# Another order of load and cast for the last four batches of an attention-then-MLP kernel

## The chip, the cores and the metric

One Trainium2 chip, one core. The metric is the device time of one execution in microseconds (us); the median over runs is compared. The engines are TensorE (PE in the profile, with its weight loads as PEld), VectorE (DVE), ScalarE (ACT), GpSimd (POOL) and SyncE (SP), whose instructions here are DMA issues. Each engine executes its own instructions in order.

## The reference

```
q, k, v: (8 batches, 8 heads, 576 tokens, 64) f32
scores = q @ k^T / 8                        # per batch and head
D[i, j] = gamma_h ** (i - j) if i >= j else 0,   gamma_h = 1 - 2 ** (-5 - h)
attn = (scores * D) @ v
x = attn.transpose(0, 2, 1, 3).reshape(4608, 512)
h = x @ w_in                                # 512 -> 2048
g = gelu_tanh(h)
out = g @ w_out                             # 2048 -> 512, f32
```

## The kernel before

The attention is computed chunk by chunk with a running state, in f16. From each batch 512 of its 576 tokens are taken in the main flow, as four chunks of 128; the last 64 tokens of every batch, the *tails*, are taken in pairs of batches and make up the ninth and last tile of the dense part. The dense part works on tiles of 512 tokens: tile t (0 to 7) is the main part of batch t, tile 8 the tails. Both dense products use a seven-product scheme on halves of the matrices, so sums of activations and weights (`x_sums`, `act_sums`) run on VectorE.

All engines' programs are written out in a fixed order by hand. A tile is a list of steps for TensorE, and `at(t, u, f)` hangs other work on step u of tile t. Three batches are in work at a time: during tile t,

- the dense layers run for batch t (`up`, `up_prod` for the first layer, `prod` for the second);
- batch t + 1 goes through attention (`scores`, `outs`); `put` copies the result from PSUM to xT, the input of tile t + 1. For the second half of the batch these copies are made on ScalarE at step 24 (line 579);
- batch t + 2 is cast from f32 to f16 in tiles whose size is one 128-token chunk of k, q or v. `parts(b)` gives the order of the 12 casts, and the list `ut` their steps, [16, 16, 17, 18, 18, 19, 20, 20, 21, 22, 22, 25]. k and q are cast on GpSimd (lines 303 and 284), v on ScalarE (line 278) for batch 4 and later. Ahead of the first one, GpSimd makes a one-element copy `gate` (line 1148) that waits for VectorE's sums of this tile. At step 24 `turn_dma` issues two DMA transposes on SP (line 333): first of all k, then of all q, into `tt`, which the scores of the next tile read. In tiles 3 to 5 the casts of k and q of a pair of tails and their own DMA transpose (line 268) follow.

The loads have one queue, SP, in the order of the list `seq`. `pump` issues from it as long as one of the `LD` = 10 staging buffers is free, and each cast frees one. A token `("h",)` at the end of a batch holds the queue until step 29 of the tile (`resume`), so that in SP's order the loads of the next batch stand behind the turns and the stores of the tile. With 10 buffers and 12 loads in a batch, the last two loads are issued only after two casts. A token `("t", b)` loads a pair of tails (`load_tails`, line 96): six DMAs of 128 KB, two each for k, q and v, into three buffers of their own. It needs no staging buffer. k and v are read in runs of 64 elements, q in runs of 128.

For tiles 2 to 5 the loads of batches 4 to 7 thus stand in SP's program as 12 loads (k0, q0, v0, k1, ... v3), then (tiles 3 to 5) the six tail loads, then the turn of k, the turn of q, the turn of the tails, and two stores of the output (line 817).

Of the kernel before, what the change touches and what calls it, by code (L numbers as in the profile page):

```python
# [20 lines left out]
def kernel(  # L21
# [11 lines left out]
    B, H, S, D = q.shape  # L33
# [95 lines left out]
    def parts(b):  # L129
        if b == NPE:  # L130
            return [(key, c) for key in "kqv" for c in range(NC)]
        return [(key, c) for c in range(NC) for key in "kqv"]

    def body(b):
        if b < NPE:
            return [("b", b, key, 2 * g + y) for g in range(2) for key in "qkv" for y in range(2)]
        return [("b", b, *x) for x in parts(b)]

    QS = (0, 2, 1, 3)
    seq = body(0) + [("i", g, ct) for g in QS for ct in range(4)]  # L140
    seq += [("o", f) for f in range(NF)] + body(1)
    TP = {4: 0, 5: 2, 6: 4, 7: 6}
    for b in range(1, B):
        seq += body(b) if b > 1 else []
        if b - 1 in TP:
            seq.append(("t", TP[b - 1]))
        if NPE <= b < 8:
            seq.append(("h",))
    q_ld = {"next": 0, "hold": False}
# [972 lines left out]
    for t in range(1, B):  # L1122
        b, tl = t + 1, TP.get(t)
# [12 lines left out]
    for b in range(NPE, B):  # L1136
        ent = parts(b)
        eng = {"k": P, "q": P, "v": P if b == NPE + 1 else A}
        t0, ut, go = b - 2, [16, 16, 17, 18, 18, 19, 20, 20, 21, 22, 22, 25], 29
        if b == NPE + 1:  # L1140
            ut = [16, 16, 17, 19, 19, 20, 22, 22, 23, 24, 24, 25]
        if b == NPE:
            t0, ut, go = 1, [0, 0, 0, 0, 2, 2, 4, 4, 6, 7, 9, 10], 12
        at(t0, ut[0], lambda b=b: (new_casts(b), new_turned(b)))
        if b >= 8:
            at(t0, ut[0], lambda: q_ld.update(hold=True))
        if b > NPE:
            at(t0, ut[0], lambda t=t0: nc.gpsimd.tensor_copy(out=gate, in_=gs[t]["2" if t in MID else "4"][:, NH - 1, 1, 0:1]))  # L1148
        for u, (key, c) in zip(ut, ent):
            at(t0, u, lambda b=b, key=key, c=c, e=eng[key]: cc(b, key, c, e))  # L1150
        at(t0, 5 if b == NPE else ut[-2] + 2, lambda b=b: turn_dma(b, TP.get(b - 1)))
        at(t0, go, resume)
# [105 lines left out]
```

## Time and profile before

The median of three runs is 285.23 us (283.83 to 286.21). The profiled execution took 283.99 us, its span is 282.2 us.

| | |
|---|---|
| PE busy | 271.8 us of the span (96%), 4106 matmuls |
| DVE busy | 234.8 us (83%) |
| ACT busy | 170.5 us (60%) |
| POOL busy | 136.4 us (48%) |
| granted TensorE clock | 0.997 |
| HBM read / written | 36.70 MB / 9.44 MB |
| DMA queue of SP | 126672 packets, 52.97 MB, 76% of 16 engines' span |

A busy share is over the whole span, with a start (the first 24 us, where PE is busy for 19.65) and an end (252.3 to 282.2 us, 25.24) that have other limits than the middle. The chain of work that ended last runs through PE for 69% of the span, DVE 11% and DMA 8%.

### The profile page before, as it was taken

Reading aid. Unit: us, or ns where it says so; the run is one execution under the profiler, and the core shown is the slowest. Engines: PE = TensorE matmul, PEld = TensorE weight load, DVE = VectorE, ACT = ScalarE, POOL = GpSimd, SP = SyncE. Lnnn points to the kernel's source line nnn. Section 1 sums busy time; section 2 is a strip of 40 time slices with the busy share of each in tenths; the row PEclk is TensorE's granted clock in tenths of the full one; section 3 lists DMA queues with packets and bytes.
Section 4 is the critical chain, followed back from the end, with each engine's and each line's share of the span. In section 5 each row is a group of like instructions: output and inputs, shape, how many; then the busy total and the mean of one; then the engine's idle time right before and its main releaser. Section 6 shows DMA issues by size and latency. Waiting matters only on the chain.

```text
span 282.2 us, 9780 instructions
## 1 busy us (share of the span) xinstructions
PE 271.8 (96%) x4106; PEld 214.5 (76%) x4106; DVE 234.8 (83%) x439; ACT 170.5 (60%) x325; POOL 136.4 (48%) x239
## 2 busy tenths in 40 slices
PE   6889999999999999999999999999999999999993
PEld 2458888888877688678867887688668877887782
DVE  6785999998968899779988997899888968875863
ACT  5477756797246864776478646874586368308800
POOL 4589809980893099109950896079717000000000
PEclk9999999999999999999999999999999999999998
DMA  6999999999979982999699999999993040012013
GB/s 196 302 385 385 379 282 242 251 208 282 226 166 264 246 204 56 269 237 222 133 214 251 205 202 194 285 206 199 192 252 68 8 153 0 2 73 78 0 39 112
DMA packets 127307, 54.11 MB, mean 192 GB/s; under 512 B 93472, under 2 KB 119072, under 8 KB 127264
## 3 DMA queue, kind: packets, MB, share of 16 engines
q1 hardware_dynamic: 126672, 52.97, 76.0%
q8 instruction: 32, 0.52, 0.9%
q10 hardware_dynamic: 592, 0.52, 0.6%
q14 instruction: 11, 0.09, 0.1%
HBM read 36.70 MB, written 9.44 MB: 163 GB/s over the span
## 4 chain that ended last, share of the span: by engine, by line
PE 69%; DVE 11%; DMA 8%; POOL 4%; ACT 3%; issue 1%; SPq 1%; DVEq 0%
PE hp L593 11%; PE opB L800 11%; PE opA L800 10%; PE opC L800 9%; PE hB L695 8%; DMA ld<-in_moe_w_in_dram 4%; PE hC L695 4%; PE opD L800 4%; PE xs L428 3%; PE hp L614 3%; POOL w_out_sb L912 2%; DMA ld<-in_q_dram 2%; PE hA L695 2%; ACT gT L710 2%; DMA ld<-in_moe_w_out_dram 2%; DVE ret L372 2%
## 5 line engine op out<-in xcount | busy, mean ns | idle before, releaser
L800 PEld LDWEIGHTS <-gT 128*128 128x128 f16 x576 | 55.0, 98 | 9.2 <-issue 0.8
L593 PE MATMUL hp<-xT,w_in_sb 128*128 128x512 f16 x192 | 49.1, 379 | 0.0
L800 PEld LDWEIGHTS <-s 128*128 128x128 f16 x432 | 42.0, 98 | 5.0
L303 POOL TENSOR_TENSOR ck<-ld,sc 128x128 f16<-128x128 f32 (+1 forms) x72 | 43.2, 626 | 1.2 <-DMA ld<-in_k_dram 0.6
L599 ACT ACTIVATE gT<-hp 128x512 f16<-128x512 f32 x48 | 28.5, 593 | 12.4 <-PE hp L593 8.9
L800 PE MATMUL opA<-w_out_sb,gT 128*128 128x256 f16 x288 | 35.0, 273 | 0.3 <-ACT w_out_sb L912 0.2
L284 POOL TENSOR_TENSOR cq<-ld,sc 128x256 f16<-128x256 f32 x48 | 31.5, 677 | 0.1
L695 PEld LDWEIGHTS <-w_in_sb 128*128 128x128 f16 x256 | 25.1, 98 | 8.2
L614 PE MATMUL hp<-xT,w_in_sb 128*128 128x256 f16 x256 | 29.7, 273 | 1.0 <-POOL w_in_sb L912 0.9
L593 PEld LDWEIGHTS <-w_in_sb 128*128 128x128 f16 x192 | 18.7, 98 | 12.8 <-DVE xT L579 0.2
L614 PEld LDWEIGHTS <-w_in_sb 128*128 128x128 f16 x256 | 24.3, 98 | 5.3 <-POOL w_in_sb L912 2.3
L710 ACT ACTIVATE gT<-k 128x512 f16<-128x512 f32 x25 | 15.8, 631 | 13.2 <-DVE k L706 13.2
L695 PEld LDWEIGHTS <-wi 128*128 128x128 f16 x192 | 18.3, 98 | 5.1
L1148 POOL COPY gate<-s 128x1 f16<-128x1 f16 x5 | 2.5, 492 | 39.1 <-DVE s L777 30.9
L776 DVE TENSOR_TENSOR s<-gT 128x512 f16<-128x512 f16 (+1 forms) x26 | 15.3, 589 | 7.2 <-ACT gT L621 4.5
L621 ACT ACTIVATE gT<-hp 128x512 f16<-128x512 f32 x32 | 18.5, 599 | 4.3 <-PE hp L614 4.1
L579 ACT CAST xT<-xs 128x512 f16<-128x512 f32 x23 | 15.4, 736 | 9.1 <-PE xs L428 9.1
L695 PE MATMUL hC<-x,w_in_sb 128*128 128x256 f16 x128 | 19.2, 273 | 0.0
L695 PE MATMUL hB<-x,wi 128*128 128x256 f16 x128 | 18.9, 273 | 0.0
L800 PE MATMUL opB<-wt,gT 128*128 128x256 f16 x144 | 18.2, 273 | 0.0
L779 DVE TENSOR_TENSOR gT<-gT 128x512 f16<-128x512 f16 (+1 forms) x26 | 17.7, 696 | 0.0
L777 DVE TENSOR_TENSOR s<-s,gT 128x512 f16<-128x512 f16 (+1 forms) x26 | 16.6, 639 | 1.2
(147 smaller groups left out, 566.7 us busy)
## 6 DMA issues: line engine op xcount, KB each, us to landing
ld<-in_q_dram SPq DMA_DIRECT2D x32, 256.0 KB, 5.4
ld<-in_k_dram SPq DMA_DIRECT2D x32, 256.0 KB, 5.7
ld<-in_v_dram SPq DMA_DIRECT2D x32, 256.0 KB, 5.3
out_dram<-ost SPq DMA_DIRECT2D x16, 512.0 KB, 4.6
ld<-in_moe_w_in_dram SPq DMA_DIRECT2D x16, 256.0 KB, 5.5
ld<-in_moe_w_out_dram SPq DMA_DIRECT2D x16, 256.0 KB, 5.7
lt<-in_k_dram SPq DMA_DIRECT2D x8, 128.0 KB, 5.7
lt<-in_q_dram SPq DMA_DIRECT2D x8, 128.0 KB, 4.7
```

The lines of the kernel that those rows point to most:

```text
L284: eng.tensor_tensor(out=a[key][:, 1024 * g + 512 * x : 1024 * g + 512 * x + 512].rearrange("p (n l d) -> p l n d", l=2, d=D)[:, y ^ x], in ...
L303: eng.tensor_tensor(out=dh[:, o], in0=x, in1=sc[:, s0, i].unsqueeze(2).to_broadcast(list(x.shape)), op=ALU.mult)
L579: cp(out=xT[:, g0 : g0 + 4 : 2].rearrange("p g n (t j) -> p g n j t", j=2), in_=t.rearrange("p (n g j t) -> p g n j t", n=HP, g=2, j=2),)
L593: nc.tensor.matmul(hp.rearrange("p (g t) -> p g t", t=TL), w_in_sb[:, ct, 128 * fc : 128 * fc + 128], xT[:, o : o + TB // TL, ct, :], star ...
L599: nc.scalar.activation(out=gT[t][:, fc].rearrange("p i n -> p (i n)"), in_=hp, func=AF.Gelu_apprx_tanh)
L614: nc.tensor.matmul(hps[n][:, 256 * x : 256 * x + 256].rearrange("p (g t) -> p g t", t=TL), w_in_sb[:, ct, 128 * (fs[n] + x) : 128 * (fs[n] ...
L621: nc.scalar.activation(out=gT[t][:, f : f + 2, 2 * u : 2 * u + 2, :].rearrange("p f i n -> p f (i n)"), in_=hp.rearrange("p (f n) -> p f n ...
L695: nc.tensor.matmul(pb[:, 256 * i : 256 * i + 256].rearrange("p (g t) -> p g t", t=TL), w(kt, i), x(kt), start=(new and i == kt == 0), stop ...
L710: due.append(lambda: nc.scalar.activation(out=g, in_=x.rearrange("p (f n) -> p f n", f=2), func=AF.Gelu_apprx_tanh))
L777: nc.vector.tensor_tensor(out=s["2"], in0=s["1"], in1=a11, op=ALU.subtract)
L779: nc.vector.tensor_tensor(out=a21, in0=a11, in1=a21, op=ALU.subtract)
L800: nc.tensor.matmul(op[tag][:, HD * u : HD * u + HD], lhs(f), rhs[:, f], start=(new and f == 0), stop=(f == NH - 1), skip_group_check=True,)
```

## The change

For batches 4 to 7 the order of the 12 loads and casts becomes k0 k1 v0 k2 k3 v1 q0 q1 q2 q3 v2 v3. The steps of the list `ut` are dealt out in that order. The token of the tail loads, which stood behind a batch's last load, is put at the eleventh place of the batch's list, between q3 and v2, for batches 5 to 7 (batch 4 has no tails; the last pair of tails is loaded elsewhere, in tile 6). Order of instructions before and after: on PE, DVE and ACT the same; on SP and POOL regrouped. Line numbers behind the change are higher by 2 or 3.

```diff
     def parts(b):
         if b == NPE:
             return [(key, c) for key in "kqv" for c in range(NC)]
+        if b >= 4:
+            return [(x[0], int(x[1])) for x in "k0 k1 v0 k2 k3 v1 q0 q1 q2 q3 v2 v3".split()]
         return [(key, c) for c in range(NC) for key in "kqv"]
...
     TP = {4: 0, 5: 2, 6: 4, 7: 6}
     for b in range(1, B):
-        seq += body(b) if b > 1 else []
+        new = body(b) if b > 1 else []
         if b - 1 in TP:
-            seq.append(("t", TP[b - 1]))
+            new.insert(10 if b < B else 0, ("t", TP[b - 1]))
+        seq += new
         if NPE <= b < 8:
             seq.append(("h",))
```

The lines of SP's program for batch 5 (tile 3), before and after:

```
before: k0 q0 v0 k1 q1 v1 k2 q2 v2 k3 q3 v3 | tails k k q q v v | turn k, turn q, turn tails | 2 stores
after:  k0 k1 v0 k2 k3 v1 q0 q1 q2 q3 | tails k k q q v v | v2 v3 | turn k, turn q, turn tails | 2 stores
```

## The prediction

> **What bounds the kernel now.** I read the busy table by stage first, then the instruction queues around one tile boundary. In what follows "tile t" is the stage that runs the two dense layers on 512 tokens of batch t; in it batch t+1 goes through attention and batch t+2 is loaded, cast and turned. The change touches batches 4 to 7, so tiles 2 to 5, which begin at 82.5, 111.1, 139.4 and 168.5 us; tile 6 begins at 197.5. The table (columns: length, then PE, PEld, DVE, ACT, POOL busy, granted clock, DMA share, GB/s):
>
> ```profile
> 111.20:139.60 28.40, 28.40 (x454) 21.82 (x452) 24.61 (x41) 18.36 (x35) 15.09 (x26) 1.00 0.93 215
> 139.60:168.50 28.90, 28.83 (x501) 22.36 (x500) 25.64 (x43) 19.04 (x37) 18.56 (x33) 1.00 0.96 213
> 168.50:197.50 29.00, 28.93 (x501) 22.52 (x500) 25.34 (x42) 19.10 (x37) 18.67 (x34) 1.00 1.03 220
> ```
>
> TensorE is never idle here: 28.40 of 28.40, 28.83 of 28.90. With the neighbouring tiles, 82.7 to 226.3 us, the idle time adds up to 0.3 us. So the change has at most 0.3 us to win there, and everything it can do beyond that is harm. The DMA share (0.93 to 1.03) says that the second resource at its limit is the DMA queue. Next, SP's queue in tile 4 (start, length of the issue, what):
>
> ```profile
> 158.15 2.71 SPq L111 DMA_DIRECT2D ld<-in_k_dram  x1
> 160.95 1.28 SPq L106 DMA_DIRECT2D ld<-in_q_dram  x1
> 162.33 0.46 SPq L111 DMA_DIRECT2D ld<-in_v_dram  x1
> 162.84 2.36 SPq L96 DMA_DIRECT2D lt<-in_k_dram  x2
> 165.24 1.31 SPq L96 DMA_DIRECT2D lt<-in_q_dram  x2
> 166.59 1.32 SPq L96 DMA_DIRECT2D lt<-in_v_dram  x2
> 168.07 3.36 SPq L333 DMA_TRANSPOSE tt<-ck  x1
> 171.53 1.99 SPq L333 DMA_TRANSPOSE tt<-cq  x1
> ```
>
> SP issues without a pause from 147.29 (the batch's first load) to 167.9: k3, q3, v3, six tail loads, then the two turns. The first ten loads are out at 160.9; the tails take 5.1 us more. Then ScalarE's timeline over the same boundary:
>
> ```profile
> 163.62 0.61 ACT L278 CAST cv<-ld 128x512 f16<-128x512 f32 x1
> 164.14 1.32 ACT L579 CAST xT<-xs 128x512 f16<-128x512 f32 x2
> 167.33 0.62 ACT L278 CAST cv<-ld 128x512 f16<-128x512 f32 x1 [1.86 <-DMA ld<-in_v_dram]
> 169.42 0.60 ACT L599 ACTIVATE gT<-hp 128x512 f16<-128x512 f32 x1 [1.48 <-PE hp L593]
> ```
>
> This is the view that decides. The cast of v2 (163.62) stands ahead of the two copies that write xT (164.14), and xT is what the first matmul of the next tile reads at 168.47. The cast of v3 already waits 1.86 us for its load (issued 162.33, so 5.0 us from issue to use), harmlessly, because it stands behind the xT copies. The program order of PE, DVE and ACT is the same before and after; only SP's and POOL's orders move.
>
> **The change, part by part.**
>
> *POOL.* The same 8 casts of k and q, regrouped: k first. In tile 4 the four k casts sum to 1.77 + 2.22 + 2.41 + 1.57 = 8.0 us and the four q casts to 5.3 us, behind the gate that ends at 156.6. So k is cast whole at 164.6 in place of 168.05, q at the same 169.5. Cost 0.
>
> *The turn of k.* It waits for k's cast, but on SP it also stands behind the loads of v2 and v3. In tile 4 SP is through with loads and tails at 167.9 in either order, and the turn is issued at 168.07 now. Gain in this tile 0.1 us, in tile 3 about 1.9 us (137.3 for 139.21). The turn of q still waits for the last q cast; its result is needed by scores some 8.6 us into the next tile, for which no PE wait is on record. Worth 0.
>
> *The loads of v2 and v3.* There are 10 staging buffers, so the last two loads of a batch wait for casts. These were q3 and v3; now they are v2 and v3. For tiles 3 to 5 the six tail loads are put ahead of them. The wait on casts (now k0 and k1) costs nothing: in tile 4 these end at 158.3 and 160.6, and also 2.6 us later (the delay worked out below) they are over before SP gets there at 166.0. What counts is the place in the queue: v2 goes from ninth load to eleventh plus six tails.
>
> *Tile 2 (no tails).* Ten loads are out at 102.3 us; v2 is issued then in place of 99.85. Landings in that window take 4.5 to 6.1 us, so it is there at 107.5 (106.8 to 108.4); its cast stands at 106.46 now. The xT copies move from 106.98 to about 108.1 and end at 109.4, before tile 3 starts at 111.1. Cost 0 us, at the worst bound 0 too (110.3); the cover is 1.7 us of ScalarE slack.
>
> *Tile 3.* Ten loads out at 129.5 (q3 is issued at 129.57 now); six tails by the rows of before 131.42 to 137.32, 5.9 us: v2 issued at 135.4. For its landing I take 4.5 us, the middle of the tail rows here (3.7 to 5.2), since it follows them in a queue that they have let drain; loads in the full queue took 4.5 to 5.7. It lands at 139.9. Then the cast (0.6), the two xT copies (1.32) and a hand-over of 0.1: tile 4 starts at 142.0 for 139.4, **+2.6 us**. The four sums of xT on VectorE (0.42 to 0.83 us each) stand behind the same copies and run beside the first matmuls, as they do at the start of tile 2 (83.24 to 85.9), where they cost PE nothing I can see. v3 follows v2 by about 0.7 us and its cast stands behind the copies: 0.
>
> *Tile 4.* Where does the delay go? SP's next loads start after the turn of q (POOL's cast end 140.7, unmoved), the tails' turn and the stores, so still at 147.3. Ten loads to 160.9, tails 5.1, v2 at 166.0, landing 4.6 (tail rows 4.2 to 4.7): 170.6; tile 5 starts at 172.7 for 168.5, **+4.2** in all, of which 1.6 are new.
>
> *Tile 5.* POOL's gate has moved by 2.6 with tile 4, and q's cast with it; SP had 1 us of slack there, so loads start 1.7 us later (178.2). Ten loads took 12.8 us, tails 5.8: v2 at 196.8, landing 4.5, tile 6 at 203.4 for 197.5: **+5.9**. Behind tile 6 no batch is loaded and nothing is given back: PE is busy 28.7 of 28.8 and 25.9 of 26.0 us in tiles 6 and 7.
>
> *Sum.* The profiled execution took 283.99 us (span 282.2 and 1.8 around it): 283.99 + 5.9 = 289.9. The runs' median, 285.23, lies 1.24 above it; the forecast of the median is 289.9 + 1.2 = **291.1 us**.
>
> *Bounds.* The unknowns are how fast the tails go when they come straight behind q3, and the landing of a load behind them. Low rows: 0.60 us for each tail issue (the shortest) and 3.7 us to land. Tile 3: 129.5 + 3.6 + 3.7 = 136.8, copies done 138.8, no loss; tile 4: 168.2, tile 5 starts at 170.3, +1.8; tile 5 adds none: 287.0 for the median. High rows: the issue lengths of before and the longest landings of a load (5.7, 6.7, 6.6): +3.8, +6.3, +9.3 with the loads of tile 5 3 us late: 294.5.
>
> **The rivals.**
>
> *The clock falls in the gaps.* The trace shows what idling costs:
>
> ```profile
> 279.00:280.00 1.00, 0.00 (x0) 0.00 (x0) 0.00 (x0) 0.00 (x0) 0.00 (x0) 1.00 1.01 318
> 280.00:281.00 1.00, 0.00 (x0) 0.00 (x0) 0.00 (x0) 0.00 (x0) 0.00 (x0) 0.83 0.56 176
> 281.00:282.20 1.20, 0.00 (x0) 0.00 (x0) 0.00 (x0) 0.00 (x0) 0.00 (x0) 0.50 0.00 0
> ```
>
> The last matmul ends at 277.66; 0.83 over one us means a drop to 0.50 at about 280.7, 3.0 us later. And a cold start, from PE's timeline:
>
> ```profile
> 2.28 3.57 PE L253 MATMUL fill<-tbb,ident 128*128 128x512 f16 x8 [2.28 <-POOL tbb L209]
> 10.40 1.47 PE L253 MATMUL fill<-tbb,ident 128*128 128x512 f16 x6
> ```
>
> Eight such matmuls took 3.57 us at first; at the later pace (0.245 each) they take 1.96: 1.6 us lost. My gaps are 2.6, 1.6 and 1.7 us, all under 3.0, so the forecast has no drop; with landings at the high rows the first gap is 3.8 and one drop follows, two at most: 294.5 + 1.6 = 296, or about 293.5 with one gap just over 3.0. The Trainium skill ("TensorE: Matmul & The Clock Gate", Part 1: The HAM clock gate) says that the clock is halved after about 3.4 us of idling, judged by a free-running window; the trace's 3.0 us agrees roughly, and by that rule also a gap of 2.6 is spared.
>
> *v2 arrives in time: not slower.* The place is the same, the copies behind v2's cast. What decides is whether v2 lands by 137.3 in tile 3 (tile 4's start of 139.4 less 2.1), 2.6 us earlier than I have it. For: the last tails are issued in 0.60 each, and a q load reads runs of twice the length of a k load's, so ten loads with four q instead of three pass sooner. Against: in all three tiles six tails took 5.1 to 5.9 us. Price as in the low bound, +0 to +1.8: 285.2 to 287.0.
>
> *The regrouping pays.* The turn of k goes out 1.9 us earlier, SP's loads of the next batch follow, and a wait for turned keys falls away. For: the DMA share is near 1. Against: PE has no such wait; the gain is capped at 0.3 us: 284.9.
>
> **How the numbers follow.** The late v2 that I forecast, +3.5 to +9.3, has a chance of 0.70 and its own range is 288.7 to 294.5; late with clock drops 0.12 (293 to 297); in time 0.15; regrouping pays 0.03. A measurement of this kernel tells about 1% (2.9 us) from no change, so slower by over 1% gets 0.82, within 1% 0.15, faster 0.03. The range runs from 286.6 (inside the in-time case) to 295.3 (into the case with the clock).
>
> **What would show it.** Right: in tiles 3 to 5 the cast of v2 on ACT with a wait of 5 to 8 us for its load; the first matmul of the next tile idle until ACT's xT copies, 2.6, then about 1.6 and 1.7 us; nothing of the kind at 111 us; the clock at 1.00 throughout; POOL's and DVE's busy time unchanged. Step by step: v2's issue at 135.4 and 166.0, the tails ahead of it. Wrong: no PE gap at the starts of tiles 4 to 6, or v2 landing under 137.3; a gap at the start of tile 3; or a PE wait on turned tiles or on xT's sums in place of the copies.

## The result and the profile after

The changed kernel takes 287.42 us (median of 12 runs, 286.1 to 291.31) for 284.39 us before (12 runs, 283.13 to 286.21). The ratio is 1.0111 with a 95% interval of 1.0092 to 1.0130: slower by 3.0 us, where +5.9 us was forecast (291.1 us for the median). The run of 291.31 us is taken as a slow one and is left out of the ratio. The profiled span is 284.8 us for 282.2 us.

The busy table by stage, with the cut and the columns shown of before:

```profile
111.20:139.60 28.40, 27.96 (x452) 21.60 (x450) 22.95 (x40) 17.86 (x35) 15.00 (x26) 1.00 0.94 204
139.60:168.50 28.90, 28.47 (x498) 22.00 (x497) 24.39 (x42) 18.57 (x37) 17.53 (x32) 1.00 1.07 218
168.50:197.50 29.00, 28.39 (x496) 21.71 (x495) 24.57 (x42) 17.64 (x35) 17.63 (x32) 1.00 0.97 214
```

TensorE, which had been idle for 0.14 us of these three stretches, is idle for 0.44, 0.43 and 0.61 us in them. The clock stays at 1.00. Cut by tiles instead (from first matmul to first matmul), tiles 2 to 6 take 28.53, 28.79, 29.63, 30.38 and 29.31 us, where before they took 28.54, 28.37, 28.88, 29.00 and 28.81. The differences add up to 3.0 us, the whole loss; tile 2 has no share in it. (The profiled span grew by only 2.6 us, because this execution came to tile 2 0.44 us earlier, at 82.08 for 82.52 us, ahead of everything that the change touches. Points in time after the change, as against those before, are early by that much from the start.)

SP's queue in tile 4, from the q loads on:

```profile
154.01 2.69 SPq L106 DMA_DIRECT2D ld<-in_q_dram  x4
156.75 1.52 SPq L96 DMA_DIRECT2D lt<-in_k_dram  x2
158.31 2.64 SPq L96 DMA_DIRECT2D lt<-in_q_dram  x2
161.06 1.42 SPq L96 DMA_DIRECT2D lt<-in_v_dram  x2
162.58 2.29 SPq L111 DMA_DIRECT2D ld<-in_v_dram  x2
164.96 4.22 SPq L336 DMA_TRANSPOSE tt<-ck  x1
169.44 1.94 SPq L336 DMA_TRANSPOSE tt<-cq  x1
```

The order is the one announced, and everything in it is early: v2 is issued at 162.58, the forecast had 166.0. ScalarE around the starts of tiles 4 (139.40) and 5 (169.03):

```profile
137.52 0.62 ACT L281 CAST cv<-ld 128x512 f16<-128x512 f32 x1 [3.47 <-DMA ld<-in_v_dram]
138.04 1.31 ACT L582 CAST xT<-xs 128x512 f16<-128x512 f32 x2
139.51 0.62 ACT L281 CAST cv<-ld 128x512 f16<-128x512 f32 x1 [0.15 <-DMA ld<-in_v_dram]
140.51 0.60 ACT L602 ACTIVATE gT<-hp 128x512 f16<-128x512 f32 x1 [0.39 <-PE hp L596]
...
143.05 0.63 ACT L713 ACTIVATE gT<-k 128x512 f16<-128x512 f32 x1 [1.24 <-DVE k L709]
...
144.07 0.58 ACT L733 COPY k<-hB 128x512 f32<-128x512 f32 x1
...
167.13 0.62 ACT L281 CAST cv<-ld 128x512 f16<-128x512 f32 x1 [3.39 <-DMA ld<-in_v_dram]
167.66 1.32 ACT L582 CAST xT<-xs 128x512 f16<-128x512 f32 x2
169.55 0.62 ACT L281 CAST cv<-ld 128x512 f16<-128x512 f32 x1 [0.58 <-DMA ld<-in_v_dram]
170.13 0.60 ACT L602 ACTIVATE gT<-hp 128x512 f16<-128x512 f32 x1
```

The cast of v2 waits for its load with the two xT copies behind it, as forecast, but for 3.4 to 4.1 us and not for 5 to 8. And two lines in the middle, the gelu that waits for VectorE and the late copy L733, belong to a second cost that the forecast did not have. TensorE shows both:

```profile
139.40 1.02 PE L596 MATMUL hp<-xT,w_in_sb 128*128 128x512 f16 x4 [0.44 <-ACT xT L582]
...
144.69 0.60 PE L698 MATMUL hB<-x,wi 128*128 128x256 f16 x4 [0.36 <-ACT k L733]
...
174.40 0.60 PE L698 MATMUL hB<-x,wi 128*128 128x256 f16 x4 [0.44 <-ACT k L733]
...
199.41 1.02 PE L596 MATMUL hp<-xT,w_in_sb 128*128 128x512 f16 x4 [0.77 <-ACT xT L582]
...
204.68 0.60 PE L698 MATMUL hB<-x,wi 128*128 128x256 f16 x4 [0.33 <-ACT k L733]
```

The first place is a tile's first matmul, idle until ACT's xT copies: the profile puts 0.44 and 0.77 us down to these copies at tiles 4 and 6. It counts from the end of the matmul before, which is modelled, so the starts of matmuls are the safer measure, and by them the gaps are somewhat longer. The last group of 16 matmuls of a tile starts 2.35, 2.01 and 2.68 us ahead of the next tile, where before it was 1.75. That is 0.60, 0.26 and 0.93 us at the starts of tiles 4, 5 and 6, 1.8 in all. The second place is 5.3 us into tiles 4, 5 and 6: 0.36, 0.44 and 0.33 us by the profile, and by the starts (0.95, 1.04 and 0.93 us from the matmuls before, for 0.44) 0.51, 0.60 and 0.50 us, 1.6 in all. Together this is 3.4 us, 0.4 more than the loss: by difference, the rest of these tiles is 0.4 us shorter than before; why stays open. The second place hangs on the first by a chain through VectorE:

```profile
139.39 0.61 DVE L673 TENSOR_TENSOR x<-xT 128x512 f16<-128x512 f16 x1 [1.45 <-ACT xT L582]
...
142.34 0.67 DVE L709 TENSOR_TENSOR k<-k,hA 128x512 f32<-128x512 f32 x1
```

VectorE stands idle for 1.45 us before the four sums of xT, which began at 138.46 before and at 139.39 now. They run one after the other, then the output sum L817, then L709 (142.34 for 141.87 before). The gelu of L713 needs that sum (143.05 for 142.59), the copy L733 stands behind it (144.07 for 143.60), and that copy frees the bank in which the matmul of 144.69 writes.

### The profile page after: what moved, and what is told of

It reads as the page before. It is cut to its first block, busy times and chain, and to the rows that moved or that the text cites. A ratio compares the mean times of both kernels' runs of the same rounds, so it can differ in the third digit from the quotient of the medians.

```text
span 284.8 us, 9784 instructions
## 1 busy us (share of the span) xinstructions
PE 271.9 (95%) x4106; PEld 213.9 (75%) x4106; DVE 231.5 (81%) x439; ACT 170.3 (60%) x325; POOL 134.3 (47%) x239
## 5 line engine op out<-in xcount | busy, mean ns | idle before, releaser
L306 POOL TENSOR_TENSOR ck<-ld,sc 128x128 f16<-128x128 f32 (+1 forms) x72 | 41.2, 607 | 1.6 <-DMA ld<-in_k_dram 1.5
L713 ACT ACTIVATE gT<-k 128x512 f16<-128x512 f32 x25 | 15.8, 632 | 15.0 <-DVE k L709 15.0
L281 ACT CAST cv<-ld 128x512 f16<-128x512 f32 x22 | 13.7, 623 | 14.8 <-DMA ld<-in_v_dram 14.8
L779 DVE TENSOR_TENSOR s<-gT 128x512 f16<-128x512 f16 (+1 forms) x26 | 14.6, 563 | 6.6 <-ACT gT L624 3.9
L803 PE MATMUL opB<-wt,s 128*128 128x256 f16 x144 | 17.4, 273 | 0.0
```

The costliest lines, as they stand in the source:

```text
L281: eng.copy(out=dst, in_=raw)
L306: eng.tensor_tensor(out=dh[:, o], in0=x, in1=sc[:, s0, i].unsqueeze(2).to_broadcast(list(x.shape)), op=ALU.mult)
L713: due.append(lambda: nc.scalar.activation(out=g, in_=x.rearrange("p (f n) -> p f n", f=2), func=AF.Gelu_apprx_tanh))
L779: nc.vector.tensor_tensor(out=s["1"], in0=a21, in1=a22, op=ALU.add)
L803: nc.tensor.matmul(op[tag][:, HD * u : HD * u + HD], lhs(f), rhs[:, f], start=(new and f == 0), stop=(f == NH - 1), skip_group_check=True,)
```

## The experiments

Theory after the result: the loss comes from v2's cast, which is late and stands ahead of the xT copies in ScalarE's order, and reaches TensorE in two places, directly and through VectorE's sums. Rivals: the reordered loads themselves (DMA or GpSimd contention), and v3's cast, which stands ahead of the next tile's first gelu. Ratios are to the kernel before, with 95% intervals; each diff is to the changed kernel, and `...` stands for code left out.

**e1_tails_last: tails behind v3 again.**

```diff
-            new.insert(10 if b < B else 0, ("t", TP[b - 1]))
+            new.append(("t", TP[b - 1]))
```

> The new order of loads and casts is kept, and only the six tail loads go back behind v3 in SP's queue (tiles 3 to 5). If the loss is v2's load standing behind the tails: v2 is issued right after q3, 6 to 7 us earlier (near 126 and 156 us), its cast on ACT waits for nothing, PE has no gap at the starts of tiles 4 to 6 nor at step 6 of these tiles, and the time is that of before, ratio to before 0.998 to 1.002. If the new order itself costs (v2 and v3 as the last two loads, q casts late), it stays near 1.011; if half and half, near 1.005.

Measured: 284.41 us, 0.9994 [0.9972, 1.0016]. v2 is issued at 130.04, 158.66 and 187.64 in tiles 3 to 5, later than expected (near 126 and 156): in tile 3 SP is through with q3 at 127.22 and stands idle until GpSimd's cast of k0 frees a staging buffer. There is still no gap at either place. The place of the tails accounts for the whole loss; the new order of loads and casts, taken together, costs nothing that these runs resolve.

**e2_v2_behind_copies: v2's cast behind the xT copies on ScalarE.**

```diff
+        if b >= 4:
+            ut = [16, 16, 17, 18, 18, 19, 20, 20, 21, 22, 24, 25]
```

> All loads and their order are as in the changed kernel; only the cast of v2 on ACT is moved from ahead of the two copies to xT to behind them (batches 4 to 7). If ACT's queue is what turns the late load into a loss: v2 lands as late as in the changed kernel (137.5, 167.1, 197.5 us, or somewhat earlier in absolute time as the tiles move up), but PE starts tiles 4 to 6 without a gap, VectorE's sums of xT wait for nothing, the gap at step 6 goes too, ratio to before 0.998 to 1.003. If the loss came from the busier DMA queue or from late turns, the ratio stays near 1.011.

Measured: 285.58 us, 1.0034 [1.0008, 1.0060]. The gaps at the starts of tiles are gone, so the first place is v2's cast ahead of the copies. What is left is a further mechanism: the late casts stand ahead of the next tile's first gelu instead. At the start of tile 5 the casts run at 168.14 and 170.01, the gelu at 170.54, and TensorE waits 0.20 and 0.45 us for the copies that free a bank (L727 and L733). The expectation that the gap 5.3 us into the tile would go too did not hold.

**e3_only_v3_behind: v2 ahead of the tails, v3 behind them.**

```diff
-            new.insert(10 if b < B else 0, ("t", TP[b - 1]))
+            new.insert(11 if b < B else 0, ("t", TP[b - 1]))
```

> The tail loads are put one place later, between v2 and v3: v2 leaves ahead of them, v3 stays behind. If only a load whose cast stands ahead of the copies to xT can hurt: no gap at the tile starts, v3's cast waits 1 to 3 us behind the copies, ratio to before 0.998 to 1.003. If any value load behind the tails costs, about half the loss remains: 1.005.

Measured: 285.93 us, 1.0045 [1.0018, 1.0071]: v3 alone costs something once it comes this late. ScalarE, then TensorE, at the start of tile 5 in this kernel:

```profile
170.36 0.62 ACT L281 CAST cv<-ld 128x512 f16<-128x512 f32 x1 [3.83 <-DMA ld<-in_v_dram]
170.88 0.59 ACT L602 ACTIVATE gT<-hp 128x512 f16<-128x512 f32 x1
171.37 0.58 ACT L727 COPY k<-hB 128x512 f32<-128x512 f32 x1
```

```profile
172.00 0.60 PE L698 MATMUL hB<-x,wi 128*128 128x256 f16 x4 [0.42 <-ACT k L727]
```

The cast waits 3.83 us, the gelu and the copy behind it follow without a pause, and TensorE waits for the bank, and again for 0.45 us at 174.34.

**e4_old_order_tails_first: the old order k0 q0 v0 ..., with the tails ahead of its last two loads.**

```diff
-        if b >= 4:
-            return [(x[0], int(x[1])) for x in "k0 k1 v0 k2 k3 v1 q0 q1 q2 q3 v2 v3".split()]
```

> The old order of loads and casts, with the tail loads ahead of the batch's last two loads (now q3 and v3). This tells the place of the tails from the order. v2 is the ninth load and early, so by the theory of v2 there is no gap at the starts of tiles 4 to 6 from the copies; q3 lands 5 to 6 us later, about when GpSimd comes to its cast (139.2 in tile 3 of before), so the turn of q is up to 2 us later and hidden: ratio 0.998 to 1.004. If tails ahead of the last two loads cost whichever these are, it is near 1.011. The ten loads with three q in them should take 12.5 to 13 us, against 10.9 to 11.5 with four.

Measured: 287.36 us, 1.0099 [1.0063, 1.0134]. The expectation that it would be hidden failed. The last two loads are q3 and v3 here, and v3's cast, harmless behind the xT copies while it waited 1.86 us, now waits 6.27:

```profile
172.89 0.62 ACT L279 CAST cv<-ld 128x512 f16<-128x512 f32 x1 [6.27 <-DMA ld<-in_v_dram]
173.42 0.59 ACT L600 ACTIVATE gT<-hp 128x512 f16<-128x512 f32 x1
173.91 0.58 ACT L725 COPY k<-hB 128x512 f32<-128x512 f32 x1
```

```profile
174.53 0.60 PE L696 MATMUL hB<-x,wi 128*128 128x256 f16 x4 [1.92 <-ACT k L725]
```

A second wait of 0.45 us follows in the same tile, and no tile starts with a gap: v3's place explains the loss here, without the late q3. Tails ahead of the last two loads cost about 1% in either order of the loads.

**e5_late_casts_next_tile: the changed kernel's loads, and the casts of v2 and v3 at step 3 of the next tile.** No cast of a late load then stands ahead of the copies or of the first gelu.

```diff
-            at(t0, u, lambda b=b, key=key, c=c, e=eng[key]: cc(b, key, c, e))
+            t1, u1 = (t0 + 1, 3) if b >= 4 and key == "v" and c > 1 else (t0, u)
+            at(t1, u1, lambda b=b, key=key, c=c, e=eng[key]: cc(b, key, c, e))
```

> Loads and their order as in the changed kernel; the casts of v2 and v3 (batches 4 to 7) move into the next tile on ACT, to step 3, behind the first gelus and copies of that tile; the values are first needed at step 15. Theory now: the late value loads cost at two places of ACT's queue, v2's cast ahead of the copies to xT, and v3's cast ahead of the next tile's first gelu. Moving v2 alone behind the copies left 0.3%. If these two places are the whole loss, no PE gap is left in tiles 4 to 6 and the ratio to before is 0.998 to 1.002. If the tails ahead of the values cost through DMA or turns as well, 1.003 to 1.005 stays.

Measured: 283.96 us, 0.9992 [0.9971, 1.0012]. The whole loss is gone with the same loads in the same order. Its busy table, cut at its own tile starts:

```profile
112.40:140.50 28.10, 28.10 (x454) 21.75 (x452) 23.88 (x41) 18.26 (x35) 14.42 (x26) 1.00 1.06 217
140.50:169.40 28.90, 28.83 (x502) 22.43 (x501) 25.06 (x43) 18.94 (x37) 18.80 (x34) 1.00 0.93 207
169.40:198.40 29.00, 28.92 (x502) 22.32 (x500) 25.30 (x43) 19.05 (x37) 18.49 (x33) 1.00 1.04 219
```

TensorE is idle for 0.15 us of the 86.0, as before the change. That rules out contention from the loads, and any cost from their lateness except through what stands behind the casts.

**e11_only_v3_next_tile: as e5, for v3 alone.**

```diff
-            at(t0, u, lambda b=b, key=key, c=c, e=eng[key]: cc(b, key, c, e))
+            t1, u1 = (t0 + 1, 3) if b >= 4 and key == "v" and c == 3 else (t0, u)
+            at(t1, u1, lambda b=b, key=key, c=c, e=eng[key]: cc(b, key, c, e))
```

> Loads as in the changed kernel; v3's cast moves into the next tile (step 3), v2's stays ahead of the copies to xT. This prices the first of the two places by itself: the PE gaps at the starts of tiles 4 to 6 stay (0.3 to 0.9 us), VectorE's sums of xT still begin late and the gaps at step 6 stay, ratio to before 1.007 to 1.011. If v3's place made more of the loss than v2's, the ratio falls to 1.005 or below.

Measured: 287.44 us, 1.0087 [1.0058, 1.0115]. v2's cast alone makes most of the loss. By the profile, gaps of 0.44, 0.29 and 0.50 us stand at the starts of tiles 4 to 6, and of 0.35, 0.24 and 0.58 at the place 5.3 us in (by the starts, 1.7 us in all at each place). So with v3's cast out of the way, the second place is still there. That it is fed by VectorE's late sums is read from the timelines; no run takes the sums out by themselves. What v3 costs in the changed kernel, 0.24% by the difference, is inside the intervals and not resolved.

**e7_four_more_loads: four more loads of 32 KB behind the tails, ahead of v2.** It makes v2 later and changes nothing else that the forecast counts.

```diff
+        x = sb.tile([128, 256], F32, tag="lx", name="lx", bufs=1) if b < TP[7] else None
+        for n in range(4 if b < TP[7] else 0):
+            nc.sync.dma_start(
+                out=x[32 * n : 32 * n + 32].rearrange("p (h d) -> p h d", d=D),
+                in_=k[b, 0:4, 32 * n : 32 * n + 32, :].rearrange("h s d -> s h d"),
+            )
```

> The changed kernel with four more small loads (32 KB each, into a buffer that nothing reads) behind the tails of tiles 3 to 5, ahead of v2: v2 is issued some 2 to 2.5 us later in each tile, so it lands about where I had forecast. If PE's loss follows v2's landing one for one, the first gap is about 2.6 us, the two others 1.5 to 2 us, span about 2.5 to 4 us longer than the changed kernel's, ratio to before 1.019 to 1.026. If the forecast's sum was wrong in its mechanism (the loss doesn't follow v2), it stays near 1.011 to 1.013.

Measured: 293.35 us, 1.0323 [1.0280, 1.0365].

```profile
143.53 1.02 PE L602 MATMUL hp<-xT,w_in_sb 128*128 128x512 f16 x4 [1.91 <-ACT xT L588]
...
174.17 1.02 PE L602 MATMUL hp<-xT,w_in_sb 128*128 128x512 f16 x4 [1.22 <-ACT xT L588]
...
205.66 1.02 PE L602 MATMUL hp<-xT,w_in_sb 128*128 128x512 f16 x4 [2.14 <-ACT xT L588]
```

Counted from the tile's start, v2's cast stands 1.5, 1.0 and 1.1 us later than in the changed kernel (28.38, 28.76, 29.61 for 26.91, 27.73, 28.50). The idle time before these matmuls, by the starts 2.1, 1.4 and 2.3 us, grew by 1.5, 1.1 and 1.4 us: close to one for one, so the rule of the forecast (a late v2 moves the next tile's start) holds, and from cast to first matmul there are 1.88 us each time. The second place did not grow with it (0.17, 0.17 and 0.23 us by the profile, for 0.36, 0.44 and 0.33). Tiles 3 to 6 took 3.5 us more than in the changed kernel, in the expected range. The whole took 5.9 us more, more than expected. In the profile tile 2 is 1.0 us longer, where the edit adds no load, and the stretch before it 1.6 us, though the start of tile 2 varies as much between kernels that don't touch it (81.8 to 83.7). The clock doesn't explain it in the profiled run (mean 0.999), though it was lower in the three others (0.982 to 0.992). This part stays open.

**e12_four_loads_behind: the same four loads behind v3,** meant as the control.

```diff
+    def load_more(b):
...
+            new.append(("x", TP[b - 1]))
...
-            if s[0] != "t":
+            if s[0] not in "tx":
...
```

> Control for the kernel with four more loads: the same four small loads into the same buffer, but behind v3 in SP's queue, ahead of the turns. v2 lands as in the changed kernel, so by the theory that the loss follows v2 the ratio is 1.009 to 1.015 (some 2 us more SP time ahead of the turns is hidden). If the extra loads or the buffer's place in memory cost by themselves, as the earlier tiles of that kernel hint (tile 2 was 1.0 us longer there, with nothing changed in it), it is near 1.02 or above.

Measured: 289.25 us, 1.0156 [1.0113, 1.0198], somewhat above what was expected. The excess over the changed kernel comes from tile 4 (32.55 us for 29.63): v2's cast waits 6.09 us there, tile 5 begins with a gap of 2.78 us, and the clock falls behind it (last section). The control was not clean. In SP's order the four loads stand ahead of the turns, k's turn goes out at 137.41 for 135.18 in the changed kernel, and tile 4's loads begin 7.1 us into the tile for 6.1.

**e6_casts_alone: loads in the old order, tails last, only the casts regrouped.**

```diff
-        if b >= 4:
-            return [(x[0], int(x[1])) for x in "k0 k1 v0 k2 k3 v1 q0 q1 q2 q3 v2 v3".split()]
...
-            new.insert(10 if b < B else 0, ("t", TP[b - 1]))
+            new.append(("t", TP[b - 1]))
...
-        ent = parts(b)
+        ent = parts(b) if b < 4 else [(x[0], int(x[1])) for x in "k0 k1 v0 k2 k3 v1 q0 q1 q2 q3 v2 v3".split()]
```

> Loads in the old order with the tails last; only the casts are regrouped (k first, then q; v2 at step 22). This tells why the next batch's loads began 1.6 to 1.8 us earlier than I had reckoned. If it is the earlier turn of k that follows from the casts: the turn of k goes out as soon as SP is through with the loads, the turn of q takes about 2 us to issue in place of 3.4 to 4.0, and k0 of the next batch is issued near 115.4 and 145.5 us relative to tile starts as in the changed kernel; ten loads still take 12.5 us or more, as three q are among them. If the early start came from the regrouped loads, it stays near 117 and 147.3. Time as before either way: ratio 0.998 to 1.002.

Measured: 284.80 us, 1.0030 [1.0002, 1.0058]. The time is 0.3% above that of before, more than expected; TensorE waits 0.64 us in tile 3 for the turned q, whose casts stand behind those of k. The early start of the next batch's loads did not come: GpSimd's casts of k wait for their loads (10.2 us in 11 waits), and the loads begin 8.0 and 7.5 us into tiles 3 and 4, for 4.8 and 6.1 in the changed kernel and 5.9 and 7.9 before. So the casts alone don't bring it. In e10 (below), with the loads alone, the loads begin 7.6 us into tile 4, but that kernel is disturbed by other waits; with both (e1) they begin 4.0 and 6.7 us in.

**e10_loads_alone: loads in the new order, tails last, casts in the old one.**

```diff
-            new.insert(10 if b < B else 0, ("t", TP[b - 1]))
+            new.append(("t", TP[b - 1]))
...
-        ent = parts(b)
+        ent = parts(b) if b < 4 else [(key, c) for c in range(NC) for key in "kqv"]
```

> Loads in the new order with the tails last, casts in the old order (v2 at step 21). Counterpart to the kernel with the casts alone: the ten loads with four q among them should go out in 10.9 to 11.5 us, and the next batch's loads should begin late as in before (117 and 147.3 us), because k's cast ends late. One look: span within 1 us of before.

Measured, in a single run: 295.66 us, span 293.9 us, far off the expectation. q0, now the seventh load, is still the second cast: GpSimd waits 3.83 us for it in tile 4 with all later casts of k behind it, and TensorE's small state matmuls wait for k, in tile 2:

```profile
109.48 0.97 PE L431 MATMUL us<-cv,ck 64*64 64x64 f16 x16 [1.70 <-POOL ck L306]
```

Again an in-order engine held up by one late load. The ten loads took 12.5, 13.3 and 11.8 us here, as in the old order, so the order of loads alone doesn't make them faster.

No version here beats the kernel before; TensorE's idle time in these tiles, 0.3 us, left nothing to gain.

## Why the prediction was right and wrong

*Right: what binds.* The direction, the place, the gaps of the first kind in tiles 4 to 6 and none in tile 3, the clock at 1.00. In tile 2 v2's cast came at 107.22 (forecast 107.5), the copies were done at 109.06 and there was no gap. That the time agrees so well is luck: v2 was issued at 100.83 and not at 102.3, and took 6.4 us from issue to cast and not 5.2. e2 and e5 show the mechanism, e7 that it pays about one for one.

*Wrong: the size of the first place, forecast at 5.9 us, measured 1.8.* The failed step is "v2 issued at 135.4" and its like in tiles 4 and 5; the terms of that sum (us; the ten loads' end includes their start):

| | tile 3: forecast, measured | tile 4 | tile 5 |
|---|---|---|---|
| loads begin | 117.0, 115.4 | 147.3, 145.5 | 178.2, 175.2 |
| ten loads out | 129.5, 126.2 | 160.9, 156.8 | 191.0, 186.7 |
| six tails take | 5.9, 7.4 | 5.1, 5.8 | 5.8, 6.5 |
| v2 issued | 135.4, 133.66 | 166.0, 162.58 | 196.8, 193.24 |
| issue to cast | 4.5, 3.9 | 4.6, 4.6 | 4.5, 4.3 |
| v2's cast | 139.9, 137.52 | 170.6, 167.13 | 201.3, 197.53 |

v2 came 2.4, 3.5 and 3.8 us earlier than forecast. Two terms of this sum were the main ones mis-sized, and both were left at the rows of before. (In tile 3 the landing was also 0.6 us too long.)

- *"Worth 0" for the turns.* With k cast first, k's turn was issued at 135.18 for 139.21 in tile 3. The forecast saw 1.9 us of this and let it end there, because q's turn waits for q's last cast. But one turn of the pair takes long to issue (last section): before, it was q's, 4.00 us from 140.72; now it is k's, 3.97 us that pass while SP waits for q's cast anyway, and q's takes 1.98 from 139.74. The tails' turn goes out at 143.04 for 144.81 and the next batch's loads begin at 145.5 for 147.3. SP's queue before, then after:

```profile
139.21 1.35 SPq L333 DMA_TRANSPOSE tt<-ck  x1
140.72 4.00 SPq L333 DMA_TRANSPOSE tt<-cq  x1
144.81 1.26 SPq L268 DMA_TRANSPOSE ett<-e  x1
...
147.29 0.92 SPq L111 DMA_DIRECT2D ld<-in_k_dram  x1
```

```profile
135.18 3.97 SPq L336 DMA_TRANSPOSE tt<-ck  x1
139.74 1.98 SPq L336 DMA_TRANSPOSE tt<-cq  x1
143.04 1.23 SPq L271 DMA_TRANSPOSE ett<-e  x1
...
145.47 2.37 SPq L111 DMA_DIRECT2D ld<-in_k_dram  x2
```

These are the 1.8 us of tile 4 in the table's first row. In tile 2 the same happens (q's turn takes 1.96 for 3.43) and the loads of tile 3 begin 1.6 us earlier, 0.45 of which the whole execution was early. This account is read from the timelines; no run changes the turns alone. The 3.0 us in tile 5 also hold the 1.7 us that the forecast added for a late tile 5.

- *"Ten loads" at 12.5, 13.6 and 12.8 us.* They took 10.9, 11.3 and 11.5; the four q loads at the end take 2.7 us together. The low rival had named this ("ten loads with four q instead of three pass sooner"), and the sum did not use it. e10 took 12.5, 13.3 and 11.8 with the same loads and the old casts, so it is not the q loads alone; e1, with loads and casts regrouped and the tails last, took 11.7, 11.6 and 11.3. What else makes them quick stays open.

The tails were slower than forecast by 1.5, 0.7 and 0.7 us, which gave part of this back. The gain of "at most 0.3 us" was right as a price on TensorE, but the earlier loads did something else: they took away a good part of the harm.

*Wrong: a cost of nothing for the four sums of xT,* which "run beside the first matmuls". They do, but the output sum, L709, a gelu and a copy follow them, and 5.3 us into the tile TensorE needs the bank which that copy frees. The start of tile 2, from which the cover was read, gives more time: TensorE runs eight matmuls first there and four in the later tiles, so that it came to this bank 5.65 us into tile 2, just behind the copy's end at 5.6, but 4.8 us into tiles 4 to 6. Now the copy ends 5.2 to 5.3 us into these. Measured by the starts: 1.6 us in the changed kernel, 1.7 in e11. The two errors have opposite signs, so the total of 3.0 us lies nearer to the forecast's 5.9 than the first place does.

*v3 at "0".* Nearly right for this kernel: its cast waits 0.15 and 0.58 us, and the next gelu (170.13, 1.10 us after the tile's first matmul) is where it was (1.11 before). It is no rule: in e3 and e4, where v3's cast waits 3.83 and 6.27 us, it holds up the first gelu (0.45% and 0.99%).

*The rivals.* In time: v2 was needed at 137.3 in tile 3 by the forecast (at 136.9 in this execution, which was earlier from the start) and came at 137.5, 0.6 us late; the first place by itself (1.8 us) lies at the top of this rival's price of 0 to 1.8; with the second the loss lies between that and the low end of the late case, 3.5. The tails, which were held against it, were even longer than forecast; it was the earlier start and the quicker ten loads that brought v2 forward. Clock: no drop in the changed kernel, with gaps of 0.9 us at most. Regrouping pays: e1 (0.9994), no.

## What to carry to other kernels

When an edit moves transfers within a queue, start each stage's sum from when the queue gets to it: by the timelines here an early turn let a long issue fall into a wait and so brought the next batch's loads forward, though nobody waited for its own result. Price a late load by what stands behind its consumer on the in-order engine, and follow that chain to the next buffer to be freed, not only to the next matmul. A cast of a late load belongs behind everything that the matmul engine will need soon: with v2 and v3 cast three steps into the next tile, the same loads cost nothing (0.9992).

## What the runs showed of the hardware

*The issue of a DMA transpose.* One held SP for 1.3 to 5.3 us in these runs. In tile 3 before, k's was issued 1.9 us after the last load and took 1.35, and q's, right behind it, 4.00; with the loads just ahead, in tile 4 before and in tiles 3 and 4 after, k's took 3.36, 3.97 and 4.22 and q's 1.94 to 1.99. So the long one of a pair seems to be the one with the most transfers just ahead of it. How full the queue is was not measured, and it is no fixed size: in tile 5 the two took 3.05 and 2.34 before, 3.43 and 3.08 after. The pair costs 5.3 to 6.5 us of SP in each of these; what the order decides is whether the long one falls into a wait.

*The clock.* In e12 it fell to 0.50 at 173.0, 1.3 us after the gap of 2.78 us had ended (columns as in the table by stage):

```profile
171.73 1.02 PE L605 MATMUL hp<-xT,w_in_sb 128*128 128x512 f16 x4 [2.78 <-ACT xT L591]
```

```profile
172.00:173.00 1.00, 1.00 (x8) 0.61 (x7) 0.97 (x2) 0.32 (x2) 0.55 (x1) 1.00 1.11 199
173.00:174.00 1.00, 1.00 (x7) 0.71 (x6) 1.00 (x4) 0.93 (x2) 0.00 (x0) 0.50 1.14 217
```

It stayed there until about 176.4, which cost some 1.7 us, an estimate from the clock in these slices (three of 0.50, one of 0.80). In e10 it fell after only 1.70 us idle between small 64x64 matmuls (and again in tile 4 after 1.60), and stayed at 0.50 for some three us while TensorE was fully busy:

```profile
110.00:111.00 1.00, 0.86 (x59) 0.70 (x59) 0.00 (x0) 0.27 (x1) 1.00 (x3) 0.89 0.84 192
111.00:112.00 1.00, 1.00 (x6) 0.75 (x5) 0.00 (x0) 1.00 (x3) 1.00 (x3) 0.50 0.36 84
```

After gaps of 1.9 and 2.1 us (by the profile) between dense matmuls (e7) it did not fall in the profiled run. So the bound of 3.0 us that the prediction read at the end of the kernel is no safe one for what comes between. Nor does the row that it read as a cold start give the price of a drop: the granted clock reads 1.00 there (2 to 6 us). The Trainium skill ("TensorE: Matmul & The Clock Gate", the closing table on why this matters) asks for no idle gaps over about 3 us; all three drops here came with shorter gaps. That the same page (Part 1: The HAM clock gate) has the clock follow how busy TensorE was within a free-running window fits e10, where sparse small matmuls lie on both sides of the gap, but no run here separates that from other reasons.
